# Block attention and a gated MLP on one core: the first pair's q and k in pieces, the ones made by GpSimd, five loads moved ahead of v, q and k

## The chip, the cores and the metric

The kernel runs on one core of a Trainium2 chip. Its time is the device time of one execution in microseconds. Before the change three runs took 744.91, 747.52 and 747.91 us; their median is 747.52 us.

The core has four computing engines and one that only issues transfers, each with its own queue of instructions that it works off in order: TensorE (PE in the profile; its weight loads are PEld), VectorE (DVE), ScalarE (ACT), GpSimd (POOL) and SyncE (SP). Transfers are issued from SP's queue, and a few from ACT's.

## The reference

Attention over 8 batches, 8 heads, 576 positions and 64 values a head, with a mask that lets a block of 64 positions see itself and all blocks before it; its output is the input x of a gated MLP.

```python
scores = scale * np.matmul(q, k.transpose(0, 1, 3, 2))
mask = block_i >= block_j            # blocks of 64
attn = softmax(np.where(mask, scores, -1e9))
x = attn @ v                         # as (8, 576, 512)

h = gelu_tanh(x @ w_in)              # 512 -> 1024
u, v = h[..., :512], h[..., 512:]
v_n = (v - mu) / np.sqrt(var + 1e-06) * g_ln
v_s = np.einsum('ts,bsd->btd', w_sg, v_n) + b_sg[None, :, None]
out = x + (u * v_s) @ w_out
```

q, k and v come as float32, w_in and w_out as float64, w_sg, b_sg and g_ln with float32 values. Nothing of what is computed changes with the change.

## The kernel before

Two heads make a **pair**; there are 32 pairs, four to a batch. A pair takes a **slot**, and slot n finishes pair n while it makes the scores and the softmax of pair n + 1, loads the v of pair n + 1 and the q and k of pair n + 2. Slots 0 to 3 are written by `opening_slot`, 4 to 7 by `middle_slot`, the rest by `slot`. From slot 4 on the products of the MLP for the batch that was finished last are put between those of the attention.

Every product is made of float32 parts in three steps: an operand x is split into a rounded part (qh, kh, xh, wi_h and so on) and the rest (ql, kl, xl, wi_l), and high by high, low by high and high by low are added up in PSUM. For q and k of a pair the split is `split_qk`: a cast, and a subtraction. From pair 1 on GpSimd does both for q and then for k. For pair 0 DVE casts q, ACT casts k, and DVE does both subtractions. `Scores.products` makes the scores s in four groups, by PE, in this order of rows of q and columns of k: q 448 to 576 by k 0 to 256, and q 64 to 192 by k 0 to 192; q 448 to 576 by k 256 to 576, and q 0 to 64 (read as columns 0 to 128) by k 0 to 64; q 320 to 448 by k 0 to 448; q 192 to 320 by k 0 to 320. In each, high by high comes first, then kh by ql, then kl by qh. DVE takes the maximum (negm) with the mask and ACT the exponent (prob). PE then turns prob by transposes into banks named pA, pB, pC, which ACT or DVE copy out (ptA, ptB, ptC), and multiplies by v into ob. PSUM has eight banks, which go round: a bank that PE writes next must have been copied out.

The weights are read once, in slots 0 to 9. `fetch(k)` issues the next k loads of a fixed list: sixteen tiles of w_in (named w; eight for the half that makes v, then eight for the half that makes u), the gain (g_bc), four tiles of w_sg (xr), the last rows of w_sg together with the bias b_sg (`fetch_ends`), and eight tiles of w_out. `weight_half` does the next part of a conversion: ACT scales the upper words of two tiles, DVE joins the words, GpSimd splits. `spatial` splits a tile of w_sg, and `layer_norm` does the named steps of the first batch's normalisation: moments m, centring c, the inverse deviation r (rs, on GpSimd) and the scaling s (vh by ACT, vl by DVE).

The order on every engine up to slot 8 is the order in which the program is written. `SCRIPT` lists, for each of slots 4 to 7, what is done at six points of the slot: behind the transposes A, behind B, behind the sums, behind the second scores, behind the split of the next q and k, and at the end. At the head of a slot stand `load_v(n + 1)` and `load_qk(n + 2)`, ahead of all that the script issues, and SP issues in that order.

At the very start come the loads of pair 0 (q on SP, k on ACT), 14 warm-up transposes on PE, constants on GpSimd, v of pair 0, the split, the loads of pair 1, two tiles of w_in, and the cast of the ones to vone; behind the first scores stand ten more warm-up transposes.

Of the kernel before, what the change touches and what calls it, by code (L numbers as in the profile page):

```python
# [9 lines left out]
F32 = mybir.dt.float32  # L10
# [4 lines left out]
ALU = mybir.AluOpType  # L15
# [5 lines left out]
def kernel(  # L21
# [13 lines left out]
    B, H, D, S = qT.shape  # L35
    P = 128
    BLK = 64
    DM = H * D
    DFF = w_in.shape[1]
    DH = DFF // 2  # L40
# [21 lines left out]
    vector = Engine("V", nc.vector)  # L62
    scalar = Engine("A", nc.scalar)
    gpsimd = Engine("G", nc.gpsimd)
    tensor = Engine("P", nc.tensor)
    sync = Engine("S", nc.sync)
# [26 lines left out]
    def copy(e, dst, src):  # L93
        f = {"v": vector.tensor_copy, "a": scalar.copy, "g": gpsimd.tensor_copy}[e]
        return f(dst, src)
# [3 lines left out]
    raw = {}  # L99
    qk = {}  # L100
    vals = {}
    v_bufs = []
    behind = {}

    def load_qk(n):
        b, h = PAIRS[n]
        q_f = sp.tile([P, S], F32, tag="q_f", name="q_f", bufs=1)
        k_f = sp.tile([P, S], F32, tag="k_f", name="k_f", bufs=1)
        sync.dma_start(q_f, qT[b, h : h + 2].rearrange("a d s -> (a d) s"))
        queue = sync if n else scalar  # L110
        ins = queue.dma_start(k_f, kT[b, h : h + 2].rearrange("a d s -> (a d) s"))
        if n:
            behind["S"] = ins
        raw[n] = (q_f, k_f)

    def split_qk(n):
        out = []
        for x, t in zip(raw.pop(n), "qk"):
            hi = sp.tile([P, S], F32R, tag=t + "h", name=t + "h", bufs=1)
            lo = sp.tile([P, S], F32R, tag=t + "l", name=t + "l", bufs=1)  # L120
            if n == 0:
                copy("v" if t == "q" else "a", hi, x)
                vector.tensor_tensor(lo, x, hi.bitcast(F32), op=ALU.subtract)
            else:
                copy("g", hi, x)
                behind["G"] = gpsimd.tensor_tensor(lo, x, hi.bitcast(F32), op=ALU.subtract)
            out += [hi, lo]
        qk[n] = out

    def load_v(n):  # L130
        b, h = PAIRS[n]
        v_f, v_d = vals[n] = v_bufs[n % 2]
        lo, hi = slice(0, BLK), slice(BLK, P)
        for a, r in ((0, lo), (1, hi)):
            cols = slice((h + a) * D, (h + a + 1) * D)
            x = v[b, : (NT - 1) * P, cols].rearrange("(j p) d -> p j d", p=P)
            if a == 0:
                sync.dma_start(v_f[:, :, r], x)
            else:
                sync.dma_start(v_f[lo, :, r], x[hi])  # L140
                sync.dma_start(v_f[hi, :, r], x[lo])
            sync.dma_start(v_d[r, : NT - 1, r], x[lo])
            sync.dma_start(v_d[r, NT - 1, r], v[b, S - TAIL :, cols])
# [24 lines left out]
    for s in (0, 1):  # L168
        t = cp.tile([P, NT - 1, 2 * D], F32, name=f"v_f{s}")
        d = cp.tile([P, NT, 2 * D], F32, name=f"v_d{s}")  # L170
        for a in (0, 1):
            r = slice(a * D, (a + 1) * D)
# [16 lines left out]
    ones = page(F32, S, "x")  # L189
# [10 lines left out]
    def fetch(k=1):  # L200

        for _ in range(k):
            coming.popleft()()
# [231 lines left out]
    Q = H // 2  # L435
# [409 lines left out]
    def weigh(k=1):  # L845

        for _ in range(k):
            weight_half()
# [6 lines left out]
    def layer_norm(*steps):  # L855

        moments, centre, inverse_std, scale = norm
        for step in steps:
            if step == "r":
                inverse_std()  # L860
            else:
                {"m": moments, "c": centre, "s": scale}[step[0]](int(step[1]))

    SCRIPT = {
        4: (
            lambda: (fetch(2), weigh(3)),
            lambda: (fetch(5), weigh(3)),
            lambda: weigh(2),
            lambda: (weigh(1), spatial(2)),
            lambda: weigh(1),  # L870
# [3 lines left out]
            lambda: (fetch(2), layer_norm("m0", "c0")),  # L874
            lambda: layer_norm("m1", "c1", "m2", "c2"),
            lambda: (layer_norm("m3"), spatial(2)),
            lambda: layer_norm("m4"),
            lambda: (layer_norm("r"), fetch(1)),
            lambda: None,
        ),  # L880
        6: (
# [17 lines left out]
    def middle_slot(n, va):  # L899

        script = SCRIPT[n]
        g = [int(x) for x in FIRST[n % Q]]
        load_v(n + 1)
        load_qk(n + 2)
        va.turn("A0")
        va.turn("A1")
        if n != 2 * Q - 2:
            split_pending()
        run_gelu()
        hole(g[0])  # L910
        script[0]()
        va.turn("B0")
        va.turn("B1")
        hole(g[1])
        script[1]()
        va.turn("C")
        va.turn_sums()
        hole(g[2])
        script[2]()
        nx = Scores(n + 1)  # L920
        nx.first()
        va.products()
        va.normalise()
        nx.second()
        if n % Q == Q - 1:
            va.split()
        else:
            pending.append(va.split)
        script[3]()
        nv = Values(n + 1, nx)  # L930
        nv.inverse()
        split_qk(n + 2)
        script[4]()
        hole(g[3])
        script[5]()
        return nx, nv

    pending = []
    last_o = []
    load_v(0)  # L940
    split_qk(0)
    load_qk(1)
    fetch(2)
    vector.tensor_copy(vone[BLK:, :], ones[BLK:, :DH])
    sc = Scores(0)
    sc.first()
    sc.second()
# [58 lines left out]
```

## Time and profile before

| | us |
|---|---|
| median of 3 runs | 747.52 |
| lowest, highest | 744.91, 747.91 |
| the profiled execution | 745.63 |
| its span, first to last instruction | 743.8 |
| PE busy | 733.2 |
| DVE busy | 463.6 |
| ACT busy | 431.0 |
| POOL busy | 295.0 |

Line numbers of the profile are those of the kernel above; nearly all instructions go through one helper and so carry its line, L60, and are told apart by the names of their tiles: out<-in, then the shape (partitions x elements). A row of a timeline has the start and the duration in us, the engine, the operation, the names, and in brackets how long the engine had been idle and what ended that. A row of the waits has who waited for whom, the total in us, how often, and the longest. A row of the stretches has the stretch, then for PE, PEld, DVE, ACT and POOL the busy time and the number of instructions, then the granted clock, the share of the transfer engines and GB/s. SPq and ACTq are the transfers that these queues issue; a transfer's own row has the KB and the median time from issue to landing.

### The profile page before, as it was taken

The numbers are of one execution on the slowest core, as the hardware profiler recorded it, in microseconds if no ns is written. First come the engines' busy times: TensorE is split into PE (matmuls) and PEld (weight loads), VectorE is DVE, ScalarE is ACT, GpSimd is POOL, SyncE is SP. The second block draws the span as 40 slices with busy tenths as digits, with TensorE's granted clock in tenths as the row PEclk, the third lists the DMA queues.
The fourth block names the chain that finished last, engine by engine and source line by source line (L and its number), as shares of the span: only waits on it lengthen the run. The fifth ranks groups of instructions, "written<-read, shape, count | busy, mean of one in ns | idle before, by whom it ended". The sixth has DMA issues, their size and how long they took to land.

```text
span 743.8 us, 18397 instructions
## 1 busy us (share of the span) xinstructions
PE 733.2 (99%) x6936; PEld 690.4 (93%) x6936; DVE 463.6 (62%) x1458; ACT 431.0 (58%) x1075; POOL 295.0 (40%) x360
## 2 busy tenths in 40 slices
PE   8998999999999999999999999999999999999998
PEld 7887989899998999989999899998999989998997
DVE  5996886578863486633966449564595446941732
ACT  5995779388643775438744587346773476712500
POOL 4766755655333343412445123453224532322121
PEclk9999999999999999999999999999999999999999
DMA  5566333343341224312252123521224221220032
GB/s 151 163 184 204 103 88 114 87 128 105 102 138 33 72 72 138 102 42 64 86 168 81 46 63 91 152 73 45 82 70 147 72 71 41 80 80 1 12 118 96
DMA packets 84299, 70.04 MB, mean 94 GB/s; under 512 B 59890, under 2 KB 59890, under 8 KB 84212
## 3 DMA queue, kind: packets, MB, share of 16 engines
q1 hardware_dynamic: 84068, 68.58, 31.4%
q8 instruction: 55, 0.90, 0.5%
q10 hardware_dynamic: 144, 0.29, 0.1%
q14 instruction: 32, 0.26, 0.1%
HBM read 49.98 MB, written 18.87 MB: 93 GB/s over the span
## 4 chain that ended last, share of the span: by engine, by line
PE 87%; DVE 5%; ACT 2%; POOL 2%; issue 2%; DMA 1%; SPq 0%; ACTq 0%; DVEq 0%; POOLq 0%
PE accs L60 16%; PE acco L60 13%; PE accv L60 13%; PE accu L60 12%; PE s L60 11%; PE ob L60 10%; PE pB L60 3%; PE pA L60 3%; PE pd L60 3%; PE pC L60 2%; ACT prob L60 2%; PE pe L60 2%; DVE prob L60 1%; DMA w<-in_w_in 1%; DVE vl L60 1%
## 5 line engine op out<-in xcount | busy, mean ns | idle before, releaser
L60 ACT ACTIVATE prob<-prob,negm 128x576 f32<-128x576 f32 (+3 forms) x320 | 176.5, 554 | 55.8 <-DVE negm L60 54.4
L60 DVE CUSTOM_DVE_ANT_0 prob<-s,mask 128x256 f32<-128x256 f32 (+3 forms) x320 | 119.3, 417 | 41.5 <-PE s L60 39.9
L60 POOL TENSOR_TENSOR xh<-x,xh 128x64 fp32r<-128x64 f32 x32 | 10.4, 324 | 196.7 <-DVE xh L60 166.5
L60 POOL TENSOR_TENSOR gl<-u,gh 128x288 fp32r<-128x288 f32 x64 | 52.0, 817 | 88.9 <-DVE gh L60 72.7
L60 PE MATMUL accu<-xh,wi_h 128*128 128x288 f32 x256 | 78.3, 306 | 0.0
L60 PE MATMUL acco<-gh,wo_h 128*128 128x288 f32 x256 | 77.5, 303 | 0.4 <-DVE negm L60 0.3
L60 PE MATMUL accs<-ws_h,vh 128*128 128x288 f32 x256 | 77.9, 304 | 0.0
L60 PE MATMUL accs<-ws_h,vl 128*128 128x288 f32 x256 | 75.5, 295 | 0.0
L60 PE MATMUL accu<-xl,wi_h 128*128 128x288 f32 x256 | 75.5, 295 | 0.0
L60 PE MATMUL accs<-ws_l,vh 128*128 128x288 f32 x256 | 75.4, 295 | 0.0
L60 PE MATMUL acco<-gh,wo_l 128*128 128x288 f32 x256 | 75.4, 295 | 0.0
L60 PE MATMUL acco<-gl,wo_h 128*128 128x288 f32 x256 | 75.4, 295 | 0.0
L60 PE MATMUL accu<-xh,wi_l 128*128 128x288 f32 x256 | 75.4, 294 | 0.0
L60 PE MATMUL s<-kh,qh 64*128 64x320 f32 (+4 forms) x384 | 65.3, 327 | 4.7 <-ACT ptC L60 2.5
L60 DVE TENSOR_TENSOR u<-accs,u 128x288 f32<-128x288 f32 x64 | 29.1, 455 | 58.5 <-PE accs L60 53.8
L60 PE MATMUL accv<-wi_h,xh 128*128 128x512 f32 x160 | 65.3, 408 | 0.0
L60 PE MATMUL accv<-wi_l,xh 128*128 128x512 f32 x160 | 62.8, 393 | 0.0
L60 PE MATMUL s<-kh,ql 64*128 64x320 f32 (+4 forms) x384 | 60.3, 305 | 0.0
L60 ACT ACTIVATION_READ_ACCUMULATOR prob<-prob,negm 128x1 f32 x320 | 60.0, 187 | 0.0
L60 PE MATMUL s<-kl,qh 64*128 64x320 f32 (+4 forms) x384 | 59.4, 305 | 0.0
L60 ACT COPY vv<-accv 128x512 f32<-128x512 f32 x32 | 18.7, 583 | 64.0 <-PE accv L60 64.0
L60 PEld LDWEIGHTS s<-kh,qh 64*128 64x128 f32 x384 | 38.2, 189 | 15.4 <-issue 6.8
(118 smaller groups left out, 2078.1 us busy)
## 6 DMA issues: line engine op xcount, KB each, us to landing
q_f<-in_qT SPq DMA_DIRECT2D x32, 288.0 KB, 3.1
spill<-x SPq DMA_DIRECT2D x32, 288.0 KB, 2.8
xr<-spill SPq DMA_DIRECT2D x32, 288.0 KB, 3.1
out_T<-xr SPq DMA_DIRECT2D x32, 288.0 KB, 3.4
k_f<-in_kT SPq DMA_DIRECT2D x31, 288.0 KB, 3.4
v_f<-in_v SPq DMA_DIRECT2D x32, 128.0 KB, 2.7
v_d<-in_v SPq DMA_DIRECT2D x64, 64.0 KB, 2.6
v_f<-in_v SPq DMA_DIRECT2D x64, 64.0 KB, 2.5
```

The source lines that it names most:

```text
L60: return lambda *a, **k: pin(method(*a, **k), self.letter)
```

## The change

Four edits:

- The first pair's q is loaded in three pieces on SP (columns 0 to 192, 448 to 576, 192 to 448) and its k in two on ACT (0 to 256, 256 to 576). Its split is done by pieces, in an order of its own over DVE and ACT.
- Of the first pair's v, head 0 is loaded ahead of the q and k of pair 1, and head 1 behind them.
- The ones are cast to vone by GpSimd instead of DVE.
- In slot 4 the last four tiles of w_in and the gain are fetched at the head of the slot, ahead of `load_v` and `load_qk`, and the two tiles of w_sg follow in the script. In slot 5 the last rows of w_sg and the bias are fetched one point earlier, ahead of the split of the next q and k.

```diff
+    Q_PARTS = slice(0, 192), slice(448, S), slice(192, 448)
+    K_PARTS = slice(0, 256), slice(256, S)
...
-        sync.dma_start(q_f, qT[b, h : h + 2].rearrange("a d s -> (a d) s"))
-        queue = sync if n else scalar
-        ins = queue.dma_start(k_f, kT[b, h : h + 2].rearrange("a d s -> (a d) s"))
-        if n:
-            behind["S"] = ins
+        if n == 0:
+            for c in Q_PARTS:
+                sync.dma_start(q_f[:, c], q[:, c])
+            for c in K_PARTS:
+                scalar.dma_start(k_f[:, c], k[:, c])
+        else:
+            sync.dma_start(q_f, q)
+            behind["S"] = sync.dma_start(k_f, k)
...
+    def split_first(x, hi, lo, c, e):
+        copy(e, hi[:, c], x[:, c])
+        return lambda: vector.tensor_tensor(lo[:, c], x[:, c], hi[:, c].bitcast(F32), op=ALU.subtract)
+
+    def split_qk_first():
+        q_f, k_f = raw[0]
+        split_qk(0)
+        qh, ql, kh, kl = qk[0]
+        (qa, qb, qc), (ka, kb) = Q_PARTS, K_PARTS
+        rest = [split_first(q_f, qh, ql, qa, "v"), split_first(q_f, qh, ql, qb, "v")]
+        split_first(k_f, kh, kl, ka, "a")()
+        for f in rest:
+            f()
+        rest = [split_first(k_f, kh, kl, kb, "a"), split_first(q_f, qh, ql, qc, "a")]
+        for f in rest:
+            f()
+
+    def load_v(n, heads=(0, 1)):
...
     SCRIPT = {
         4: (
+            lambda: weigh(3),
             lambda: (fetch(2), weigh(3)),
-            lambda: (fetch(5), weigh(3)),
...
-            lambda: layer_norm("m4"),
-            lambda: (layer_norm("r"), fetch(1)),
+            lambda: (layer_norm("m4"), fetch(1)),
+            lambda: layer_norm("r"),
...
+        if n == Q:
+            fetch(5)
         load_v(n + 1)
         load_qk(n + 2)
...
-    load_v(0)
-    split_qk(0)
+    load_v(0, (0,))
+    split_qk_first()
     load_qk(1)
+    load_v(0, (1,))
     fetch(2)
-    vector.tensor_copy(vone[BLK:, :], ones[BLK:, :DH])
+    gpsimd.tensor_copy(vone[BLK:, :], ones[BLK:, :DH])
```

`split_qk(0)` now only makes the tiles. PE's order is the same before and after. Three places where the order of other engines differs follow.

DVE's first instructions, up to the first maximum, before:

```order
L60 CAST qh<-q_f 128x576
L60 TENSOR_TENSOR ql<-q_f,qh 128x576
L60 TENSOR_TENSOR kl<-k_f,kh 128x576
L60 CAST vone<-x 64x512
L60 ISA prob_110,negm<-s,mask 128x256
```

and with the change:

```order
L60 CAST qh<-q_f 128x192
L60 CAST qh<-q_f 128x128
L60 TENSOR_TENSOR kl<-k_f,kh 128x256
L60 TENSOR_TENSOR ql<-q_f,qh 128x192
L60 TENSOR_TENSOR ql<-q_f,qh 128x128
L60 TENSOR_TENSOR kl<-k_f,kh 128x320
L60 TENSOR_TENSOR ql<-q_f,qh 128x256
L60 ISA prob_113,negm<-s,mask 128x256
```

Three whole operations became seven on pieces, the cast of the ones has gone to GpSimd, and ACT, which had one cast of k, has the casts of two pieces of k and of q's last piece.

SP's queue at the head of slot 4, from the last tiles that slot 3 fetches (the spill is slot 3's output), before:

```order
L60 DMA w<-in_w_in 128x256 x4
L60 DMA spill<-x 128x576
L60 DMA v_f_102<-in_v 128x4x64
...
L60 DMA q_f<-in_qT 128x576
L60 DMA k_f<-in_kT 128x576
L60 DMA w<-in_w_in 128x256 x4
L60 DMA g_bc<-in_g_ln 128x512
L60 DMA xr<-in_w_sgT 128x576 x2
```

and with the change:

```order
L60 DMA w<-in_w_in 128x256 x4
L60 DMA spill<-x 128x576
L60 DMA w<-in_w_in 128x256 x4
L60 DMA g_bc<-in_g_ln 128x512
L60 DMA v_f_105<-in_v 128x4x64
...
L60 DMA q_f<-in_qT 128x576
L60 DMA k_f<-in_kT 128x576
L60 DMA xr<-in_w_sgT 128x576 x2
```

Four tiles of w_in and the gain have moved past the seven loads of v and those of q and k; the two w_sg tiles stay behind them.

GpSimd's queue at the end of slot 5 (xr is the tile for the bias, q and k are those of pair 7):

```order
 L60 MEMSET sums 128x2
-L60 CAST qh<-q_f 128x576
-L60 TENSOR_TENSOR ql<-q_f,qh 128x576
-L60 CAST kh<-k_f 128x576
-L60 TENSOR_TENSOR kl<-k_f,kh 128x576
-L60 TENSOR_SCALAR rs<-stats 128x5
-L60 TENSOR_TENSOR rs<-rs,half 128x5
 L60 MEMSET xr 64x576
+L60 CAST qh<-q_f 128x576
+L60 TENSOR_TENSOR ql<-q_f,qh 128x576
+L60 CAST kh<-k_f 128x576
+L60 TENSOR_TENSOR kl<-k_f,kh 128x576
```

The zeroing of the bias tile, and with it the bias' loads, moved ahead of the split of pair 7 and of the two rs operations.

More of the change, by code (lines that the diff above doesn't have):

```diff
@@ L108, in load_qk @@
         k_f = sp.tile([P, S], F32, tag="k_f", name="k_f", bufs=1)
-        sync.dma_start(q_f, qT[b, h : h + 2].rearrange("a d s -> (a d) s"))
-        queue = sync if n else scalar
-        ins = queue.dma_start(k_f, kT[b, h : h + 2].rearrange("a d s -> (a d) s"))
-        if n:
-            behind["S"] = ins
+        q = qT[b, h : h + 2].rearrange("a d s -> (a d) s")
+        k = kT[b, h : h + 2].rearrange("a d s -> (a d) s")
+        if n == 0:
[6 more added lines that the diff above has]
+            behind["S"] = sync.dma_start(k_f, k)
         raw[n] = (q_f, k_f)
@@ L120, in split_qk @@
             lo = sp.tile([P, S], F32R, tag=t + "l", name=t + "l", bufs=1)
[L121 to L124, printed above, removed]
+            if n:
                 copy("g", hi, x)
@@ L128, in split_qk @@
         qk[n] = out
-    def load_v(n):
+    def split_first(x, hi, lo, c, e):
[14 more added lines that the diff above has]
+    def load_v(n, heads=(0, 1)):
         b, h = PAIRS[n]
@@ L133, in load_v @@
         lo, hi = slice(0, BLK), slice(BLK, P)
-        for a, r in ((0, lo), (1, hi)):
+        for a in heads:
+            r = (lo, hi)[a]
             cols = slice((h + a) * D, (h + a + 1) * D)
```

## The prediction

> **What bounds the kernel now.** I read the page's busy shares first, then the busy time by stretch, then who TensorE (PE) waits for, and last the timelines around those waits.
>
> ```profile
> PE 733.2 (99%) x6936; PEld 690.4 (93%) x6936; DVE 463.6 (62%) x1458; ACT 431.0 (58%) x1075; POOL 295.0 (40%) x360
> ...
> 58.00:69.00 11.00, 8.46 (x56) 6.89 (x54) 6.78 (x16) 5.14 (x13) 6.53 (x7) 1.00 0.82 239
> 130.00:175.00 45.00, 45.00 (x413) 41.35 (x413) 31.07 (x92) 28.38 (x73) 23.80 (x33) 1.00 0.33 98
> 307.00:397.00 90.00, 90.00 (x868) 85.40 (x866) 53.52 (x175) 52.64 (x131) 32.29 (x38) 1.00 0.30 86
> ```
>
> PE bounds the whole: 733.2 us of the 743.8 us span. From 130 us on it is busy without a break (45.00 of 45.00, 90.00 of 90.00), so nothing in the loop can be won by other engines, and a microsecond saved before 130 us should reach the end whole. What is left to save lies in PE's waits, all early:
>
> ```profile
> PE s L60 <- ACT ptC L60: 2.5, 1, 2.5
> PE s L60 <- DVE ql L60: 1.5, 1, 1.5
> PE s L60 <- DVE negm L60: 0.6, 2, 0.3
> PE ob L60 <- DMA v_f<-in_v: 0.3, 1, 0.3
> ```
>
> The change addresses three places: the opening (the 1.5), slot 4 (the 2.5, in 58 to 69 us) and slots 5 and 6 (the 0.6 and the 0.3).
>
> **Opening.** The chain is load, split, scores.
>
> ```profile
> 0.72 0.41 ACTq L60 DMA_DIRECT2D k_f<-in_kT  x1
> 0.72 0.39 SPq L60 DMA_DIRECT2D q_f<-in_qT  x1
> 1.35 3.25 PE L60 MATMUL warm<-ident 128*128 128x128 f32 x14 [1.35 <-POOL ident masks.py:199]
> 4.88 0.46 DVE L60 CAST qh<-q_f 128x576 fp32r<-128x576 f32 x1 [4.88 <-DMA q_f<-in_qT]
> 5.38 0.76 DVE L60 TENSOR_TENSOR ql<-q_f,qh 128x576 fp32r<-128x576 f32 x1
> 5.41 0.67 ACT L60 CAST kh<-k_f 128x576 fp32r<-128x576 f32 x1 [2.97 <-DMA k_f<-in_kT]
> 6.11 0.76 DVE L60 TENSOR_TENSOR kl<-k_f,kh 128x576 fp32r<-128x576 f32 x1
> 6.51 0.42 PE L60 MATMUL s<-kh,ql 64*128 64x256 f32 x2
> 6.92 0.58 PE L60 MATMUL s<-kl,qh 64*128 64x256 f32 x2
> 7.30 0.36 PE L60 MATMUL s<-kh,qh 64*128 64x192 f32 x2
> ...
> v_f<-in_v SPq DMA_DIRECT2D x32, 128.0 KB, 2.7
> ...
> L60 DVE TENSOR_TENSOR u<-accs,u 128x288 f32<-128x288 f32 x64 | 29.1, 455 | 58.5 <-PE accs L60 53.8
> ```
>
> Whole q is usable 4.16 us after its issue (4.88 - 0.72), whole k 4.69 (5.41 - 0.72). PE gets its second product at 6.51 when ql is done (5.38 + 0.76 = 6.14), its third at 6.92 when kl is (6.87), and leaves the first group at 7.30.
>
> After the change the first group needs q's columns 64 to 192 and 448 to 576 and k's 0 to 256: the first two q pieces (96 and 64 KB) and the first k piece (128 KB), half the bytes. Their landing is not in the trace. Bounds: at best as v's 128 KB, 2.7 us, so 0.72 + 2.7 = 3.4; at worst with the whole transfers, 4.88 and 5.41. I take 3.9 for the first pieces, since the same bytes of q and k go out together and half are there about halfway, and 4.4 for the second.
>
> The splits, from 0.76 us at 576 columns and 0.455 at 288, cost VectorE (DVE) about 0.15 us plus 1.06 ns a column: kl 256 takes 0.42, ql 192 0.35, ql 128 0.29, and casts about 0.2. ScalarE (ACT) does kh 256 in about 0.35 (0.67 at 576). So kh at 4.25; qh's second piece at 4.6; then in DVE's queue kl to 5.0, ql to 5.35 and ql to 5.65. The second product starts near 5.7, the third follows 0.2 later without a wait, and PE leaves the group near 6.1: 1.2 us before 7.30. The rest, kl 320 and ql 256, ends near 6.6, and PE asks for it later. With the best landing it is 1.8; with the worst, the last ql ends at 5.41 + 0.35 + 0.42 + 0.35 + 0.29 = 6.82 and PE leaves near 7.2, no gain, or 0.3 lost to five more instructions on two queues.
>
> Does it reach the next slot? Three paths must move with it:
>
> ```profile
> 11.44 2.01 PE L60 MATMUL warm<-ident 128*128 128x128 f32 x10
> 13.29 1.04 PE L60 MATMUL pA<-ident,prob 128*128 128x128 f32 x8
> ...
> 11.61 0.66 POOL L60 CAST qh<-q_f 128x576 fp32r<-128x576 f32 x1 [7.06 <-PE s L60]
> 14.47 1.41 POOL L60 TENSOR_TENSOR kl<-k_f,kh 128x576 fp32r<-128x576 f32 x1
> ```
>
> GpSimd (POOL) starts the second pair's split when PE has read the first (11.61) and its kl ends at 15.88, where PE takes it: this moves by the same 1.2 if that pair's q has landed, and its load is now ahead of v's second head. ACT's exponents follow DVE. PE itself is the third. Its warm-up matmuls go at 0.23 us each (14 in 3.25) and pA at 0.13 (8 in 1.04), while the granted clock reads 1.00 in every stretch: the pace changes near 12.8 us, inside the ten. If it changes at that same moment, work moved ahead of it runs at the slow pace and PE's own path gains 0.8 only; if continuous scores bring it forward, it holds nothing back. I keep 1.2, bounds -0.3 and 1.8.
>
> The Trainium skill, "TensorE: Matmul & The Clock Gate", Part 1, states that the array runs at half rate until a free-running window of about 3.4 us was busy throughout. The trace's two paces agree (0.23 against 0.13). By that rule the gap of 1.5 us that closes would bring the full pace one window earlier, and the opening would give about 0.4 more.
>
> The ones' cast moves to POOL, idle for 7.06 us there; on DVE it stood before a wait for PE. It costs nothing; without that cover it would be about the 0.66 of the cast above.
>
> **Slot 4.** The last weight tiles are issued behind v, q and k.
>
> ```profile
> 52.10 1.95 SPq L60 DMA_DIRECT2D w<-in_w_in  x4
> 54.15 0.38 SPq L60 DMA_DIRECT2D spill<-x  x1
> 62.31 1.81 SPq L60 DMA_DIRECT2D w<-in_w_in  x4
> ...
> 60.60 0.43 ACT L60 ACTIVATE w<-w 128x256 f32<-128x256 f32 x1 [0.34 <-DMA w<-in_w_in]
> 61.41 0.59 ACT L60 COPY vv<-accv 128x512 f32<-128x512 f32 x1
> 67.41 0.97 ACT L60 ACTIVATE w<-w 128x256 f32<-128x256 f32 x2 [5.41 <-DMA w<-in_w_in]
> 68.29 0.57 ACT L60 COPY ptC<-pC 128x512 f32<-128x512 f32 x1
> ...
> 68.91 0.41 PE L60 MATMUL s<-kh,qh 64*128 64x320 f32 x1 [2.54 <-ACT ptC L60]
> ```
>
> The tiles go out at 62.31 and ACT, which has no other work ahead, stands 5.41 us for them. Behind it in ACT's queue is the copy of pC, which frees the bank that PE needs at 66.4 (68.91 - 2.54). Issued right behind the spill, at 54.6, the tiles come 7.7 us earlier. They took 5.1 us here (67.41 - 62.31); behind four others they may take 7 (the fourth of 52.10, issued near 53.7, was waited for until 60.60), so 61.7. ACT gets to them at 62.0. The pages that they take were last read in slots 2 and 3, so no new wait stands there. Even at twice 5.1 they land at 64.9, and pC is copied by about 66.4. The whole 2.5 is won; bounds 2.0 and 2.6. DVE, 3.67 us idle for the same tiles, moves with it.
>
> What is late next: v, q and k of later slots now lie behind five transfers of 256 KB, 5.5 us at the 239 GB/s of 58 to 69 us. The two w_sg tiles (xr) had all of these ahead of them before as well, so they land as before, by 72.02 at the latest.
>
> ```profile
> 72.02 0.67 POOL L60 CAST ws_h<-xr 128x576 fp32r<-128x576 f32 x1
> 76.27 0.66 POOL L60 CAST qh<-q_f 128x576 fp32r<-128x576 f32 x1
> 93.11 0.67 POOL L60 CAST qh<-q_f 128x576 fp32r<-128x576 f32 x1 [3.43 <-PE s L60]
> ...
> 86.81 0.39 PE L60 MATMUL s<-kh,qh 64*128 64x256 f32 x2
> ```
>
> POOL reaches w_sg earlier (69.5), may wait there until 72.02 and is then where it was before, while PE runs 2.5 us ahead. POOL's slack of 3.43 us at 93.11 covers that, and the seventh pair's split, begun at 76.27 and 4.3 us long (11.61 to 15.88 above), is done at 80.6, ahead of PE's 86.81 - 2.5 = 84.3.
>
> **Slots 5 and 6.** The zeroed tile for the bias stands behind a split on POOL.
>
> ```profile
> 99.08 0.57 POOL L60 MEMSET xr<- 64x576 f32 x1
> 99.68 0.61 SPq L60 DMA_DIRECT2D xr<-in_b_sg  x2
> 101.42 0.67 ACT L60 CAST ws_l<-xr 64x576 fp32r<-64x576 f32 x1 [1.62 <-DMA xr<-in_b_sg]
> 102.12 0.75 DVE L60 TENSOR_TENSOR ws_l<-xr,ws_l 1x576 fp32r<-1x576 f32 x1 [2.31 <-ACT ws_l L60]
> ```
>
> Ahead of that split the memset runs in POOL's 3.43 us of idle time, and the bias lands before ACT asks. ACT wins 1.62 us, DVE as much, and PE its waits on negm and ob: 0.6 + 0.3 = 0.9, bounds 0.4 and 0.9.
>
> **Sum.** 1.2 + 2.5 + 0.9 = 4.6 us: span 743.8 - 4.6 = 739.2. The profiled execution took 745.63, so 741.0. The runs shown are 744.91, 747.52 and 747.91; with the profiled one their mean is 746.5, from which I take the sum: **741.9 us**.
>
> **Rivals.**
> 1. The opening gives nothing: pieces land with the whole, or the pace holds PE. For it: the first 288 KB took over 4 us where others take about 3. Against it: half the bytes decide. 746.5 - 3.4 = 743.1.
> 2. Slot 4's wait is replaced: the tiles land after 66, or another bank or tile ends last. For it: DMA is at 0.82 in 58 to 69 us. Against it: 66.4 is 4 us after the tiles' 61.7. Left are 1.2 + 0.9: 746.5 - 2.1 = 744.4.
> 3. Slower: the w_sg tiles, last in SP's queue, hold POOL, and the split of the seventh pair behind them holds PE. That split ends 8.5 us after the first w_sg tile lands (76.27 - 72.02, and 4.3) and PE wants it at 84.3, so it decides when the tile lands after 75.8. For it: v, q and k stand ahead. Against it: at most 72.02. At 85 us it is 746.5 - 4.6 + 9.2 = 751.1.
> 4. The edits cancel or PE hides other waits: 746.5.
>
> **How the numbers follow.** Forecast 0.55, rivals 0.24, 0.12, 0.05 and 0.04. The sum's bounds are 2.1 (-0.3 + 2.0 + 0.4) and 5.3 (1.8 + 2.6 + 0.9), so 744.4 to 741.2; with 2 us below and 0.6 above for the scatter of the runs shown, the range is 738.9 to 745.0; it holds rivals 1 and 2. About 0.5% (3.7 us) is what a measurement can tell: faster takes most of the forecast (0.50) and half of rival 1 (0.12), with a little of rival 2, 0.63; within 0.5% the rest, 0.31; slower 0.06.
>
> **What would show it.** Right: PE's second score product near 5.7 and kl of the second pair near 14.7; no PE wait on ptC in slot 4 and no ACT wait of 5 us on w; no ACT wait on the bias; PE's busy time unchanged and the span near 739. Wrong: the first casts still near 4.9; a wait of ACT or PE on w in slot 4; POOL waiting on xr with PE behind it on kl; or PE waits that reappear before 130 us.

## The result, and the profile after

The changed kernel takes **739.57 us** (median of six executions, 739.48 to 740.26), the kernel before in the same comparison 745.81 us (743.35 to 747.91): a ratio of 0.9917 with a 95% interval of 0.9896 to 0.9938. Forecast were 741.9 us and 738.9 to 745.0. The profiled execution took 739.77 us with a span of 738.0, against 745.63 and 743.8.

The busy times of the changed kernel, which answer to the first line that the prediction quotes of the page:

```profile
PE 730.3 (99%) x6936; PEld 687.4 (93%) x6936; DVE 466.2 (63%) x1461; ACT 431.6 (58%) x1077; POOL 296.0 (40%) x361
```

PE is as much the bound as before, with the same 6936 products, but busy for 2.9 us less. Its longest waits now (who waits for whom, total us, how often, longest):

```profile
PE s L60 <- DVE negm L60: 0.5, 2, 0.3
```

The waits on ptC (2.5), on ql (1.5) and on v_f (0.3) are gone; nothing over 0.5 is left but the very first. The two waits on negm, which were to go, are still there. Where the time went is read best from the same products in both traces. The stretches below are cut at the same four products in each: slot 0's second scores, the end of slot 3 (the first transpose of rx), the first product of the MLP behind slot 4's scores, PE's end. Columns: stretch, length, then busy time (and instructions) of PE, PEld, DVE, ACT, POOL, the granted clock, the share of the transfer engines, GB/s. First the kernel before:

```profile
0.00:15.56 15.56, 12.68 (x80) 11.37 (x80) 8.01 (x30) 8.56 (x24) 7.44 (x22) 1.00 0.55 145
15.56:48.38 32.82, 32.50 (x409) 27.83 (x408) 30.41 (x114) 28.59 (x87) 22.20 (x28) 1.00 0.63 177
48.38:73.96 25.58, 23.00 (x240) 19.70 (x240) 19.35 (x67) 18.20 (x53) 16.48 (x19) 1.00 0.66 196
73.96:740.30 666.34, 664.99 (x6212) 631.49 (x6210) 405.41 (x1249) 375.61 (x915) 248.92 (x294) 1.00 0.29 85
```

and the changed kernel:

```profile
0.00:12.93 12.93, 10.71 (x80) 8.82 (x80) 8.54 (x34) 8.68 (x26) 8.13 (x23) 1.00 0.58 157
12.93:46.31 33.38, 32.63 (x408) 27.84 (x408) 31.05 (x113) 29.01 (x88) 22.25 (x28) 1.00 0.67 182
46.31:68.91 22.60, 22.57 (x240) 19.54 (x240) 19.22 (x67) 18.08 (x52) 14.74 (x17) 1.00 0.74 217
68.91:734.30 665.39, 664.38 (x6212) 631.22 (x6210) 406.93 (x1250) 375.83 (x915) 250.91 (x295) 1.00 0.29 85
```

- **Opening:** 15.56 - 12.93 = 2.63 us. Of that PE's busy time gives 1.97 (12.68 - 10.71, the same 80 products at a higher pace) and its idle time 0.66.
- **Slots 1 to 3:** 0.56 is given back (33.38 - 32.82), most of it as idle time of PE (0.32 before, 0.75 after) at the end of slot 3.
- **Slot 4:** 25.58 - 22.60 = 2.98; PE's idle time falls from 2.58 to 0.03.
- **From there on:** 666.34 - 665.39 = 0.95. By the same products, 0.39 are won at slot 5's last scores and 0.58 in slot 6, and 0.02 lost ahead of them.

The sum is 6.0 us. The opening's timeline (start, duration, engine, names; in brackets idle time and releaser), with PE's rows first, then DVE's, ACT's and POOL's:

```profile
4.52 0.58 PE L60 MATMUL s<-kh,qh 64*128 64x256 f32 x2
4.90 0.49 PE L60 MATMUL s<-kh,ql 64*128 64x256 f32 x2
5.36 0.26 PE L60 MATMUL s<-kh,qh 64*128 64x192 f32 x2
7.60 1.32 PE L60 MATMUL warm<-ident 128*128 128x128 f32 x10
...
3.24 0.65 DVE L60 CAST qh<-q_f 128x192 fp32r<-128x192 f32 x2 [3.24 <-DMA q_f<-in_qT]
...
3.44 0.41 ACT L60 CAST kh<-k_f 128x256 fp32r<-128x256 f32 x1 [0.51 <-DMA k_f<-in_kT]
...
11.93 1.41 POOL L60 TENSOR_TENSOR kl<-k_f,kh 128x576 fp32r<-128x576 f32 x1
```

The first casts start at 3.24 and 3.44 instead of 4.88 and 5.41, the second product at 4.90 instead of 6.51. PE reaches the second half of the first group at 5.36 (7.30 before) without having stood between the warm-ups and the scores, and ten warm-ups take 1.32 us instead of 2.01: the full pace is there by 7.60 (by the trace's clock record from 5.26 on), where before it came at 12.92. Slot 4, by the same columns, ACT first, then PE, then POOL:

```profile
57.65 0.43 ACT L60 ACTIVATE w<-w 128x256 f32<-128x256 f32 x1 [1.08 <-DMA w<-in_w_in]
60.56 0.84 ACT L60 ACTIVATE w<-w 128x256 f32<-128x256 f32 x2
61.31 0.57 ACT L60 COPY ptC<-pC 128x512 f32<-128x512 f32 x1
...
63.95 0.33 PE L60 MATMUL s<-kh,qh 64*128 64x320 f32 x2
...
68.97 0.67 POOL L60 CAST ws_h<-xr 128x576 fp32r<-128x576 f32 x1 [1.83 <-DMA xr<-in_w_sgT]
```

ACT's 5.41 us for the tiles have shrunk to 1.08, its copy of pC is done at 61.88, and both heads' products of the second group start together at 63.95; before, one started at 66.05 and the other at 68.91. GpSimd does wait for w_sg, but only until 68.97.

Slots 5 and 6, PE's rows, the kernel before:

```profile
92.01 0.74 PE L60 MATMUL s<-kh,qh 64*128 64x320 f32 x2
104.88 1.16 PE L60 MATMUL ob<-ptA,v_f 128*64 128x128 f32 x16 [0.27 <-DMA v_f<-in_v]
109.08 0.38 PE L60 MATMUL s<-kh,qh 64*128 64x320 f32 x1 [0.34 <-DVE negm L60]
109.70 0.38 PE L60 MATMUL s<-kh,qh 64*128 64x320 f32 x1 [0.24 <-DVE negm L60]
```

and the changed kernel:

```profile
86.98 0.35 PE L60 MATMUL s<-kh,qh 64*128 64x320 f32 x2
103.07 0.38 PE L60 MATMUL s<-kh,qh 64*128 64x320 f32 x1 [0.31 <-DVE negm L60]
103.69 0.38 PE L60 MATMUL s<-kh,qh 64*128 64x320 f32 x1 [0.24 <-DVE negm L60]
```

The 0.39 come at the first of these rows: before, the second head's product started 0.39 us behind the first one's. The 0.58 come in slot 6, up to the waits on negm, which have 0.55 us instead of 0.58.

### The profile page after: what moved, and what is told of

Same layout as the page of the kernel before. It is cut to its first block, busy times and chain, and to the rows that moved or that the text cites. A ratio compares the mean times of both kernels' runs of the same rounds, so it can differ in the third digit from the quotient of the medians.

```text
span 738.0 us, 18412 instructions
## 1 busy us (share of the span) xinstructions
PE 730.3 (99%) x6936; PEld 687.4 (93%) x6936; DVE 466.2 (63%) x1461; ACT 431.6 (58%) x1077; POOL 296.0 (40%) x361
## 4 chain that ended last, share of the span: by engine, by line
PE 89%; DVE 6%; ACT 2%; issue 1%; DMA 1%; POOL 0%; SPq 0%; ACTq 0%; DVEq 0%
PE accs L60 16%; PE accv L60 14%; PE acco L60 13%; PE accu L60 12%; PE s L60 10%; PE ob L60 10%; PE pA L60 3%; PE pB L60 3%; PE pd L60 3%; ACT prob L60 2%; PE pC L60 2%; PE pe L60 2%; DVE prob L60 2%; DVE vl L60 1%; DMA q_f<-in_qT 0%
## 5 line engine op out<-in xcount | busy, mean ns | idle before, releaser
L60 PE MATMUL s<-kh,qh 64*128 64x320 f32 (+4 forms) x384 | 63.4, 322 | 0.5 <-DVE negm L60 0.5
L60 POOL CAST kh<-k_f 128x576 fp32r<-128x576 f32 x31 | 20.7, 667 | 75.7 <-PE s L60 75.7
```

The source lines that it names most:

```text
L60: return lambda *a, **k: pin(method(*a, **k), self.letter)
```

## The experiments

All were timed in five rounds, four kernels or fewer at a time, beside the kernel before on the same chip: 746.74 us for the first four, 746.38 for the next four, 746.94 for the filled one, 745.21 for the last three. Together the kernel before was executed 74 times there (median 746.28, from 742.46 to 749.69). The changed kernel itself was timed only in the first comparison (above) and with the last three; where others are set against it, the times come from two comparisons.

### One part of the change alone

The opening alone: the loads, `split_first` and `split_qk_first`, the order of v and the cast of the ones, as the change has them. The five fetches of slot 4 alone:

```diff
     SCRIPT = {
         4: (
+            lambda: weigh(3),
             lambda: (fetch(2), weigh(3)),
-            lambda: (fetch(5), weigh(3)),
...
+        if n == Q:
+            fetch(5)
         load_v(n + 1)
```

The bias alone:

```diff
-            lambda: layer_norm("m4"),
-            lambda: (layer_norm("r"), fetch(1)),
+            lambda: (layer_norm("m4"), fetch(1)),
+            lambda: layer_norm("r"),
```

And, in the kernel before, warm-ups that fill the whole wait for the first scores:

```diff
-    warm(bank("warm"), 14)
+    warm(bank("warm"), 24)
```

The opening:

> The change's opening alone (q and k in pieces, the new split order, the second pair's loads ahead of v's second head, the ones by GpSimd); slots 4 and 5 as before. If the three places add up (theory A), it wins what PE's matmuls were ahead at the entry of slot 4 with the whole change, 2.1 us: 745.8 - 2.1 = 743.7, ratio 0.997; the score product of slot 4 behind ptC still waits some 2.5 us. If the opening was gained only because slot 4 lets it pass (rival B: slot 4's wait on the weight tiles ends at a time of the transfers' own), it wins under 0.7 and that wait grows by what the opening won. PE's pace changes near 5 us as in the changed kernel.

Slot 4:

> The kernel before with the five fetches at the head of slot 4 alone. Theory A: 2.5 to 2.9 us won, 745.8 - 2.7 = 743.1, no PE wait on ptC, and ACT's wait on w under 1 us. Rival: the tiles came early only since the opening was earlier; then 0 to 1 us won. Its opening is that of the kernel before, so its profile shows once more when PE's pace changes there: near 12.8 us if that is fixed by the work, elsewhere if it is a window with a phase of its own.

The bias:

> The kernel before with the bias fetch one point earlier in slot 5 alone. Theory A: 0.9 us won (745.8 - 0.9 = 744.9, ratio 0.999), no ACT wait on the bias and no PE wait on negm near 109 us. Rival: DVE's chain is late for another reason and PE still waits; 0 won. Its profile shows the pace of the opening of before a further time.

The warm-ups:

> The kernel before with 24 instead of 14 warm-up transposes ahead of the first scores, so that PE has no gap of 1.5 us there; nothing else. If PE's pace rises after some 3.5 us of unbroken work (theory P), it rises near 5 us as in the changed kernel, the first scores take half as long, and about 1 us is won: 744.8, and the runs scatter less than the 4.5 us of before. If the pace has nothing to do with the gap, it still rises near 12.8, the added transposes delay the scores by about 0.4, and the time is 745.8 to 746.2.

| kernel | median, us | executions | ratio to before |
|---|---|---|---|
| opening alone | 744.28 | 743.08 to 747.95 | 0.9982 (0.9964 to 0.9999) |
| slot 4 alone | 741.32 | 740.91 to 741.61 | 0.9928 (0.9911 to 0.9945) |
| bias alone | 745.21 | 741.10 to 749.64 | 0.9981 (0.9960 to 1.0003) |
| 24 warm-ups | 746.01 | 743.41 to 748.39 | 0.9993 (0.9975 to 1.0011) |

Only slot 4's interval is well clear of 1. The opening's ends at 0.9999, and those of the bias and of the warm-ups hold 1, so these two medians show nothing by themselves. Measured by what was expected, the opening gave 2.5 us by its median (2.1 expected), though its profiled execution (745.57) is hardly better than that of the kernel before; slot 4 gave twice the 2.5 to 2.9; with the bias alone the waits on negm, which were to go, stayed (0.5 us); and the 24 warm-ups brought the pace forward to 7.04 us, not to 5, and won neither the 1 us nor the smaller scatter.

The bias' profile does show its part: in slot 6 its PE gains 0.63 us on the kernel before, and the four kernels without that edit (opening alone, slot 4 alone, 24 warm-ups, and the filled one below) gain nothing there (-0.10 to 0.00). The 0.39 at slot 5's last scores are not the bias': slot 4 alone and the 24 warm-ups have them too (0.43 each).

Against their common 746.74 the parts give 2.5, 5.4 and 1.5 us, together 9.4; the whole change gave 6.2 in its own comparison. One reason for the excess shows in the two kernels in which the wait of slot 4 is left beside a changed opening. PE's wait there with the opening alone:

```profile
PE s L60 <- ACT ptC L60: 1.6, 1, 1.6
```

and with 24 warm-ups, where PE comes to it earlier:

```profile
PE s L60 <- ACT ptC L60: 3.2, 1, 3.2
```

Behind that wait something else follows. Stretches of 3.41 us, laid along the places where the trace's clock record changes (same columns as above; the number behind the five engines is the granted clock). The opening alone:

```profile
64.58:67.99 3.41, 1.78 (x26) 1.51 (x25) 2.27 (x5) 2.33 (x6) 0.23 (x1) 1.00 0.96 324
67.99:71.40 3.41, 3.41 (x39) 3.41 (x40) 2.59 (x17) 2.92 (x10) 3.06 (x5) 0.50 0.23 88
```

24 warm-ups:

```profile
65.07:68.48 3.41, 0.30 (x5) 0.07 (x1) 1.32 (x4) 1.28 (x4) 0.00 (x0) 1.00 0.86 289
68.48:71.89 3.41, 3.30 (x27) 3.23 (x29) 3.31 (x15) 2.91 (x9) 2.09 (x4) 0.50 0.48 186
71.90:75.31 3.41, 3.41 (x44) 3.41 (x42) 0.22 (x4) 1.80 (x8) 3.25 (x4) 0.50 0.02 5
```

and the kernel before, whose profiled execution stood 2.5 us but not within one such stretch:

```profile
64.12:67.53 3.41, 2.25 (x19) 1.54 (x17) 0.13 (x1) 0.12 (x1) 1.57 (x2) 1.00 0.90 282
67.53:70.94 3.41, 2.03 (x33) 1.99 (x35) 3.20 (x12) 2.85 (x7) 0.79 (x2) 1.00 0.87 297
```

A window in which PE was busy for 1.78 or 0.30 of 3.41 us is followed by one or two windows at half clock; windows with 2.25 and 2.03 are not. With the opening alone PE was 1.86 us ahead of the kernel before behind the wait and 0.22 ahead after the half window, so that window ate 1.6; with 24 warm-ups PE was 0.32 ahead behind the wait and 2.84 behind past the two windows. The Trainium skill, "TensorE: Matmul & The Clock Gate", Part 1, has a window of 3413 ns that runs free of the kernel; the records here change at steps of 3.413 us and start at another phase in each execution, as it says. The same page of the Trainium skill puts the fall behind a whole idle window, and, in "Why this matters for your kernels", warns of gaps over about 3 us. The trace of the opening alone shows it behind a gap of 1.6 us that lies inside one window.

The slot 4 edit alone has no such stretch in its profile, and its six times lie within 0.7 us of each other. Four of the six have a mean clock of 0.997 and take no longer (741.25 us on average, the other two 741.26). Where their half windows fell isn't shown; that one in the opening need not cost anything is seen further down. The mean clock is a rough measure for a second reason: the clock record begins with the first rise, so the half pace ahead of it isn't counted.

### Is it the wait that lowers the clock?

First, work in place of idleness: in the kernel before, 40 transposes that nobody reads, between the first two groups of scores in slot 4.

```diff
     def products(self, *parts):
...
+            for _ in range(self.fill):
+                tensor.transpose(self.last[:, 448:512], ident[:BLK, :], ident[:BLK, :BLK])
+            self.fill = 0
...
         nx = Scores(n + 1)
+        if n == Q:
+            nx.fill = 40
```

> The kernel before with 40 small transposes (64 columns each, their result is not used) put on TensorE in slot 4 between the first and the second group of scores, where it stands for pC's copy: together about 2.3 us of work where the profile of before stood 2.5 us. TensorE then is not idle there, though it does nothing useful. Theory (the wait by itself costs what the profile shows, and the rest of the slot 4 edit's 5.4 us comes from the clock, which falls to half behind that wait in many executions): the stretch of half clock behind slot 4 is gone, the time lies within about 1 us from run to run instead of 742 to 748, at 744 to 746 us, where the fetch alone had 741.3. Rival (the scatter and the extra loss come from when the w_in tiles land, not from the clock): the scatter of 742 to 748 us stays, with a median of 746 us or more, since the fill adds work where the wait was shorter than it.

It took 747.09 us (745.73 to 748.78), a ratio of 1.0005 (0.9991 to 1.0019). By the numbers the theory missed: the time did not fall, and the scatter of 3 us stayed. In its profile the fill takes the wait's place (PE is 0.3 us ahead of the kernel before behind it) and no half clock follows; a mean clock of 0.998 or less, which 50 of the 74 executions of the kernel before have, was left in 4 of 12. Those 4 took 747.68 to 748.78 us, the others 745.73 to 747.41. So a lower clock became rarer, as the theory has it, but the executions without it are no better than those of the kernel before: a fill of 2.3 us costs what it exceeds the wait by, and the wait was 1.6 and 1.8 us in two other profiles. The median is also what the rival expects, by which the scatter comes from the landing of the tiles. That landing does vary: ACT starts on the last tiles at 67.41 us in the kernel before, at 65.52 with the opening alone, 67.06 with 24 warm-ups and 66.30 here. How the two shares divide wasn't measured.

Then the reverse: the changed kernel with a stall put back, by copying pC ten or seven times more on ACT (the same values into the same tile), and the changed kernel itself beside them.

```diff
+            if which == "C" and self.n == Q:
+                for _ in range(10):
+                    copy("a", pt, t)
             copy("a" if which == "C" and self.n < 2 * Q else TE[which], pt, t)
```

Ten copies:

> The changed kernel with the stall of slot 4 put back and nothing else: ScalarE copies pC ten times more (0.47 us each, the same values again) ahead of the copy that frees the bank, so that TensorE, which in the changed kernel takes that bank at 63.95 us with 2.1 us to spare, should stand there for about 2.6 us (61.31 + 10 x 0.47 + 0.57 = 66.6). The transfers stay as the changed kernel has them. Theory (such a stall by itself sends the clock to half behind it in many executions): the stall costs more than its length; half of the executions or more have a mean granted clock of 0.998 or less, the median is 743 to 745 us and the times lie 2.5 us or more apart. Rival (the stall costs its length, and the scatter of the kernel before and the rest of the gain come from the transfers or elsewhere): 739.6 + 2.6 = 742.2 us within 0.5, the times within 1 us of each other, the mean clock 0.999 or 1.0.

Seven:

> As the changed kernel with the stall put back, but with seven more copies of pC instead of ten, so that TensorE should stand there for about 1.2 us (65.2 - 63.95). Theory (the clock falls behind the stall): if 1.2 us are enough for it, the median lies 2 us or more above 739.6 with single executions near 743; if it takes a longer stall, 740.8 us within 0.4 and no executions of a lower clock. Rival (the stall costs its length): 740.8 us within 0.4 too, and then the kernel with 2.6 us has 742.2.

The changed kernel again:

> The changed kernel itself, on the same chip as the two with the stall put back, to compare them with. Both theories: 739.6 us within 0.4, all times within 1 us of each other, and the mean granted clock 0.999 or 1.0. A wider scatter would say that the small scatter of its first six executions was chance, and that the half clock is not tied to slot 4's stall.

| kernel | median, us | executions |
|---|---|---|
| ten copies | 742.33 | 741.46 to 744.25 |
| seven copies | 739.71 | 739.58 to 740.29 |
| the changed kernel | 739.52 | 739.45 to 740.81 |

No execution of the three has a mean clock below 0.999. The ten copies cost 2.8 us, which is the rival's number; but their times lie 2.8 us apart too, where the rival had 1, without any lowered clock. So part of such scatter has another source than the clock. And the stall was not the one that was meant: the scores went on at 63.70 while the copies ran until 66.85, so they hadn't been given pC's bank, and PE waited later and for less, for rb, which stands behind the copies in ACT's queue. The wait of PE with ten copies:

```profile
PE ob L60 <- ACT rb L60: 1.5, 1, 1.5
```

and the window with that wait, in the trace's own grid:

```profile
64.56:67.97 3.41, 1.93 (x34) 1.65 (x33) 1.89 (x14) 3.31 (x7) 1.89 (x3) 1.00 0.70 249
```

PE was busy for 1.93 of 3.41 us, more than in the two windows that a fall followed. It fits the account by windows, in which a stall counts by what falls into one of them, and does not prove it: the stall of 2.6 us that was to be tested did not come about. The seven copies caused no new wait of PE and cost 0.2 us, where both sides had 1.2; they tell nothing apart. The changed kernel repeated itself: 12 executions in two comparisons lie between 739.45 and 740.81 us, all with a mean clock of 0.999 or 1.0.

What the 74 executions of the kernel before say: the 24 with a mean clock of 0.999 or 1.0 have a median of 744.8 us, the 50 with 0.998 or less one of 747.2. (One window at half clock takes 3.41 / 2 / 744 = 0.0023 from the mean, two take 0.0046.) A lowered clock thus goes with about 2.4 us in two executions of three. It is no simple rule: the 27 with 0.995 or less all took 745.64 us or more, but among the 23 with 0.997 or 0.998 are five of the six fastest of all (742.46 to 743.72). That the half clock stems from slot 4 in each of them isn't shown, since only profiled executions have a trace, and slot 4 alone, which has the same opening and not the wait, has 0.997 in four of six.

### What the opening's gain consists of

Both undo a part within the changed kernel. Seven first warm-ups instead of fourteen open the gap before the first scores again:

```diff
-    warm(bank("warm"), 14)
+    warm(bank("warm"), 7)
```

> The changed kernel with 7 instead of 14 of the first warm-up transposes, so that TensorE stands idle again for about 1.6 us ahead of its first scores, as it did before the change (7 x 0.23 us are taken away). Theory (the closed gap brings TensorE's fast pace forward): in the changed kernel the pace rises at 5.26 us, with the gap it rises one window of about 3.4 us later or more, so the warm-ups, pA and the scores up to then run at half pace; TensorE reaches slot 0's second scores 0.5 to 1.5 us later than the 12.93 us of the changed kernel, and the median is 740.1 to 740.6 us against 739.6. Rival (the gap does not matter, only when the first pieces land and are split): first scores at 4.5 us, second scores at 12.9 us, median 739.6 within 0.3 us.

It took 740.42 us (740.14 to 740.79): **0.85 more** than the changed kernel, as the theory had it. PE's rows:

```profile
4.26 0.58 PE L60 MATMUL s<-kh,qh 64*128 64x256 f32 x2 [1.16 <-DVE qh L60]
5.96 0.42 PE L60 MATMUL s<-kl,qh 64*128 64x192 f32 x2
```

The first scores come earlier (4.26; there are fewer warm-ups ahead), but a product of 192 columns takes 0.42 us where the changed kernel has 0.27 at that place, and the pace rises at 9.15 instead of 5.26. The windows ahead of the rise, changed kernel first:

```profile
1.85:5.26 3.41, 3.41 (x19) 3.06 (x19) 1.91 (x6) 2.09 (x4) 3.15 (x11) 1.00 0.85 229
```

and with seven warm-ups:

```profile
2.33:5.73 3.40, 2.09 (x12) 1.42 (x12) 2.36 (x7) 1.88 (x4) 3.01 (x8) 1.00 0.80 213
5.74:9.14 3.40, 3.40 (x30) 3.28 (x28) 3.01 (x19) 1.79 (x6) 0.00 (x0) 1.00 0.56 174
```

In these two the pace rises behind the first window that PE filled, which is the rule of that page of the Trainium skill. (Ahead of the first entry of the clock record these rows show 1.00 whatever the pace.) Other traces don't fit it as neatly: with whole loads the pace rose behind a window with 3.24 us of work, all of it warm-ups, and in the kernel before it did not rise behind one with 3.38 us, all of it scores (6.09 to 9.51). That the rise comes earlier goes with the changed opening: in the seven profiles that have the changed opening whole it comes at 4.22 to 9.97 us, in the four with the opening of before at 10.22 to 13.44.

Then whole loads, with the splits still in pieces:

```diff
-            for c in Q_PARTS:
-                sync.dma_start(q_f[:, c], q[:, c])
-            for c in K_PARTS:
-                scalar.dma_start(k_f[:, c], k[:, c])
+            sync.dma_start(q_f, q)
+            scalar.dma_start(k_f, k)
```

> The changed kernel with the first pair's q and k loaded whole, one transfer each, while the splits stay in pieces. Theory (the pieces' earlier landing is what the opening wins): the first casts go back from 3.24 us to between 4.7 and 5.4 us, the first scores from 4.52 to near 6, and TensorE reaches the second scores 1.2 to 1.8 us later than 12.93; the median is 740.8 to 741.4 us against 739.6, near that of the kernel with the slot 4 fetch alone plus the bias fetch (741.3 - 0.95 = 740.4) or above. Rival (splitting in pieces is the gain, the landing is not): first casts near 4.9 us but the first group ends within 0.6 us of the changed kernel, median 739.6 to 740.1 us.

It took 741.31 us (740.48 to 741.69): **1.7 more**, the theory's number. With whole loads, DVE and ACT:

```profile
4.75 0.57 DVE L60 CAST qh<-q_f 128x192 fp32r<-128x192 f32 x2 [4.75 <-DMA q_f<-in_qT]
...
5.10 0.77 ACT L60 CAST kh<-k_f 128x256 fp32r<-128x256 f32 x2 [2.65 <-DMA k_f<-in_kT]
```

The landing goes back to 4.75 and 5.10 and the second product to 6.49, the 6.51 of before: splitting in pieces alone wins nothing there. Two windows of the same execution:

```profile
4.78:8.18 3.40, 2.08 (x28) 1.86 (x30) 2.90 (x12) 1.07 (x3) 0.39 (x2) 1.00 0.04 9
8.19:11.59 3.40, 3.40 (x21) 3.00 (x18) 3.40 (x19) 3.32 (x13) 1.36 (x2) 0.50 0.80 230
```

The pace was full from 4.77, fell to half behind a window with 2.08 us of work, and rose again at 11.60. The first was busier than two others that no fall followed (2.03 and 1.93), so the busy share that the profile shows is not the whole rule. This execution, with a half window in its opening, was the fastest of the six.

### The 0.56 us given back in slots 1 to 3

DVE and POOL at the end of slot 3, kernel before:

```profile
46.48 0.84 DVE L60 TENSOR_SCALAR r<-sums 128x10 f32<-128x10 f32 x1
...
46.00 1.29 POOL L60 TENSOR_TENSOR wi_l<-w,wi_h 128x512 fp32r<-128x512 f32 x1
```

and the changed kernel at the ends of slots 2 and 3:

```profile
33.78 0.16 DVE L60 TENSOR_SCALAR r<-sums 128x10 f32<-128x10 f32 x1
34.11 1.31 DVE L60 CAST xh<-x 128x576 fp32r<-128x576 f32 x1
44.17 1.07 DVE L60 TENSOR_SCALAR r<-sums 128x10 f32<-128x10 f32 x1
45.41 0.40 DVE L60 CAST xh<-x 128x576 fp32r<-128x576 f32 x1
...
33.82 1.29 POOL L60 TENSOR_TENSOR wi_l<-w,wi_h 128x512 fp32r<-128x512 f32 x1
43.93 1.28 POOL L60 TENSOR_TENSOR wi_l<-w,wi_h 128x512 fp32r<-128x512 f32 x1
```

The addition of 1e-9 to ten sums takes 0.16 us or up to 1.07, the cast of xh 0.40 or 1.31; the long ones end behind GpSimd's subtraction (45.24 after 45.21, 35.42 after 35.11). In the kernel before the addition met the subtraction too (0.84 here, 0.63 in slot 2), only later in its course. The loss for PE lies in one place: its lead over the kernel before is 2.53 us at the scores just ahead and 2.07 at the transposes of rx, which need this addition; the long cast in slot 2 cost it nothing. And it isn't in every execution: in the second profile of the changed kernel the addition takes 0.22 us there and PE loses nothing. The Trainium skill, "SBUF — State Buffer", section "SBUF: two separate sides", calls the port pair that VectorE and GpSimd share an exclusive lock, under which, for some of VectorE's operations, the later one stands until the other has ended; the rows agree. Two kernels try to get around it:

```diff
-            vector.tensor_scalar_add(r, self.sm.rearrange("p i a -> p (i a)"), 1e-9)
-            vector.reciprocal(r, r)
+            vector.reciprocal(r, self.sm.rearrange("p i a -> p (i a)"))
```

> The changed kernel with DVE's addition of 1e-9 to the softmax sums left out (the reciprocal reads the sums themselves; the sums are at least 1, so the float32 value is the same). That addition took 0.16 us where GpSimd was idle and 1.07 us in slot 3, ending with GpSimd's subtraction for wi_l. Theory (in slots 1 to 3 DVE's one-input operations wait for a GpSimd operation that is under way, which gives 0.6 us of the opening's gain back): the next one-input operation of DVE, the cast of xh, meets the same GpSimd operation, so that the wait moves to it and TensorE wins only 0 to 0.3 us by the end of slot 3; median 739.3 to 739.6 us. Rival (the 0.9 us belong to the addition itself): all of it goes, TensorE is 0.6 us earlier at the end of slot 3 and the median is near 739.0 us.

The second has in addition, in `opening_slot`, `split_pending()` behind the softmax of the next pair's first rows instead of ahead of it. What that moves is the split of x (the cast of xh on DVE and the rest on GpSimd), not that of w_in's words, as the text on record has it.

> As the kernel without the addition of 1e-9 to the softmax sums (left out here too), and in slots 0 to 3 the pending split of w_in's words on GpSimd is issued after the softmax of the next pair's first rows instead of ahead of it, so that GpSimd's long subtraction no longer runs beside DVE's small operations at the slot's end. Theory (DVE waits for GpSimd's operation): the DVE operations around the sums take their short times again (cast of xh near 0.4 us instead of 1.31 in slot 2), and TensorE keeps the 0.6 us that it gave back between slot 0 and the end of slot 3: median near 739.0 us. Rival (something else takes the 0.6 us, the split being needed by then or another wait behind it): TensorE's lead at the end of slot 3 stays near that of the changed kernel, median 739.4 to 739.9 us.

Without the addition, in all 32 slots: 738.93 us (738.01 to 740.14), **0.6 less** than the changed kernel, near the rival's number. DVE and POOL in slot 2:

```profile
34.01 0.40 DVE L60 CAST xh<-x 128x576 fp32r<-128x576 f32 x1
...
32.80 1.28 POOL L60 TENSOR_TENSOR wi_l<-w,wi_h 128x512 fp32r<-128x512 f32 x1
```

The wait did not move to the cast: it is short again because GpSimd's subtraction comes 1.0 us earlier and is all but over when DVE gets there. PE is 0.47 us further ahead at the end of slot 3, but 0.34 at slot 4's first scores. In this profile (1.8 us below the changed kernel's) most of the gain comes later: the two waits on negm in slot 6 are gone (0.46), and 1.0 more comes behind. So the 0.6 of the medians aren't shown to be those of slot 3. It is the shortest time of all kernels here, but its six executions overlap with the changed kernel's. With the split of x moved: 739.83 us (738.89 to 740.17), the rival's case: in slot 2 the cast of xh comes only at 37.86, it is short (0.45), and PE's lead at the end of slot 3 is the changed kernel's within 0.02 us.

## Why the prediction was right, and where it was off

**The direction and the places were right.** The opening and slot 4 gained where they were said to, slots 5 and 6 in part elsewhere, and the time lies in the range, 0.7 us above its lower end. (That end is 738.9 as written; by the prediction's own sum, 741.2 - 2, it would be 739.2, which holds the time too.)

| part | forecast (bounds), us | by the two profiles, us |
|---|---|---|
| opening | 1.2 (-0.3 to 1.8) | 2.63 at slot 0's second scores, 2.07 at the end of slot 3 |
| slot 4 | 2.5 (2.0 to 2.6) | 2.98 |
| slots 5 and 6 | 0.9 (0.4 to 0.9) | 0.95, of which 0.58 by the bias |
| sum | 4.6 (2.1 to 5.3) | 6.0 |

**Opening, mis-sized at two terms.** The first pieces were set at 3.9 us; they are there at 3.24 and 3.44, as early as the best bound (3.4), k's first cast is done at 3.85 instead of 4.25, and the second product started at 4.90 instead of 5.7. Two readings of the lines were wrong, without changing much: 7.30 is not where PE leaves the first group but its second half (it left at 7.89), and the second product at 6.51 did not wait for ql, which was done at 6.14; it followed the first by 0.38 us as in the changed kernel (4.52, 4.90). And the pace was held out of the sum ("I keep 1.2"). It gave 1.97 us of the 2.63 in this profile; by medians closing the gap is worth 0.85 us (seven warm-ups) and the earlier landing 1.7 (whole loads). By the page of the Trainium skill that was weighed there 0.4 us were to be added; the sign was right, and the size less than measured. But how much arrives varies from one execution to the next: in the second profile of the changed kernel the pace rose at 9.48, PE was 2.2 us later in the first scores, 1.0 at slot 0's second scores, and, since it lost nothing to the addition, only 0.4 at the end of slot 3. The step "PE itself is the third path" also missed DVE's addition behind GpSimd's subtraction, which took 0.46 back in the first profile. The pair's kl on GpSimd was expected near 14.7; it starts at 11.93 and ends at 13.34.

**Slot 4, right in mechanism, under-sized twice.** ACT's wait for the tiles and PE's for ptC are gone, and the tiles were ready when ACT asked for the last of them at 60.56 (61.7 was estimated). The wait was counted from the end of the last product, 66.37, to 68.91. But the products of two heads start together when they can; the held one could have started beside the other at 66.05, which makes 2.86. What was missing altogether is the clock behind the wait. "The granted clock reads 1.00 in every stretch" was true of the one profile; with half clock behind the wait it cost 1.6 us more in one other profile and 3.2 in another. The w_sg tiles, "late next", came at 68.97, earlier than the bound of 72.02: rival 3 had no ground.

**Slots 5 and 6, the right size by luck.** Of the 0.9, 0.6 were the waits on negm. They stayed: 0.58 us before, 0.55 after, and 0.5 with the bias alone. What went is the wait on v_f (0.27), as forecast, and gaps that stand in no row of waits, in which a second head's product was held behind the first: 0.39 at slot 5's last scores, which other kernels without the bias edit win too, and the rest of slot 6's 0.58.

**PE's busy time unchanged: wrong.** It fell from 733.2 to 730.3 us, 1.97 of it in the opening. Products at half pace count as busy, so an edit can shorten the work itself.

**The start of the sum.** It was taken from 746.5, the mean of four times, not from the profiled 745.63. That lifted the forecast by 0.9 us. From 745.63 the measured 6.0 us lead to 739.6, the median. That the other three times were longer by a lowered clock, which the change removes, is likely from the executions above and not shown for these three. So of the 2.3 us by which 741.9 was too high, 0.9 are the starting point, 0.9 the opening, 0.5 slot 4, and the rest slots 5 and 6 and rounding.

**The rivals.** None came true. The opening's gain did vanish in part where slot 4 was left alone (of PE's lead of 1.73 us at slot 0's second scores, 0.22 was left behind slot 4, and 1.64 of the loss came in the half window), through the clock, which no rival had named.

## What to carry to other kernels

A wait of the bounding engine can cost more than its length: in two of the four profiles with slot 4's wait the clock fell behind it. Look at the scatter of the times and at the mean clock of single executions, not at one profile alone: 4.5 to 6 us of scatter within one comparison before, 1.4 us in all 12 executions after. Count a saving from the execution whose profile was read, look whether the work itself runs at its full pace in the stretch that is shortened, and look whether a wait that was counted is the wait that went. When DVE's small operations move in time, look at what GpSimd does at the new place: an operation of 0.16 us took up to 1.07.

## What was not expected of the hardware

- One stall of 1.6 us in slot 4 was followed by 3.41 us of TensorE at half clock, one of 3.2 us by 6.83. Stalls of 2.5, 1.8 and 1.5 us, spread over two windows or with more work beside them, were not.
- The clock's rise in the opening came at 5.26, 9.48 or, with a gap, 9.15 and 12.92 us; the record changes at steps of 3.413 us from a phase that differs from one execution to the next.
- What counts as work in such a window stays open: windows with PE busy for 0.30, 1.78 and 2.08 of 3.41 us were followed by half clock, windows with 1.93, 2.03 and 2.25 were not; the pace rose behind one with 3.24 and not behind one with 3.38.
